# Seven block products per two batches in an attention and mixer kernel, with the last weights rounded a pair earlier

## The chip, the cores and the metric

The kernel runs on one core of a Trainium2 chip. The time is device microseconds (us) of one execution. Engines are named as in the profile: PE (matmuls), PEld (PE's weight loads), DVE (VectorE), ACT (ScalarE), POOL (GpSimd) and SP, whose queue issues nearly all transfers. Each engine works through its own queue in order and waits on semaphores that other engines raise.

## The reference

```python
def _attn_ref(q, k, v, centroids):          # batch 4, 8 heads, 768 tokens, head size 64
    ...
    mask = q_assign[:, :, :, None] == k_assign[:, :, None, :]
    scores = scale * np.matmul(q, k.transpose(0, 1, 3, 2))
    scores = np.where(mask, scores, -1000000000.0)
    ...
    return np.matmul(attn, v).astype(np.float32)

def _moe_ref(x, w_tok1, w_tok2, w_ch1, w_ch2):   # 768x256, 256x768, 512x1536, 1536x512
    xt = x.transpose(0, 2, 1)
    h = np.maximum(xt @ w_tok1, 0.0) @ w_tok2
    u = x + h.transpose(0, 2, 1)
    h2 = np.maximum(u @ w_ch1, 0.0) @ w_ch2
    return (u + h2).astype(np.float32)
```

Everything is float32. The output of the attention, with the heads side by side, is the `x` (768 tokens by 512) of the mixer.

## The kernel before

The program has three stretches, all written out by hand in one order; nothing is reordered afterwards, so the text of the program is the order of each engine's queue.

**Attention** (up to about 318 us): 16 pairs of heads, `g` = 0 to 15, four pairs for each batch. Of a pair, PE makes scores (line 422), ACT the exponentials (429), DVE adds them up (437), PE multiplies with v (447), ACT copies the result out (454), a transposing transfer turns it (459), and in the next pair ACT puts it into `x` (`pair_put`, 472) and DVE divides (`pair_out`, 498). Beside this the mixer's weights are loaded and rounded (`weight_steps`), in pieces of 128 by 512 words of 8 bytes. One piece is: a load into `raw` on SP (197), two ACT operations (203: `wh`, 205: `wup`), three DVE operations (210, 215, 220, the last writing `wT`), and an integer add on POOL (227) that writes the weight. A step of the list takes the load of piece i, the ACT part of piece i-1 and the rest of piece i-2. The first three weights (19 pieces) are finished in pair 14; the 12 pieces of the last one, `ch2`, begin in pair 15.

**Tokens** (318 to 401 us). `tok1(b, t)`: six matmuls of 512 columns into one bank (527), then a ReLU into `h1s[b][:, t]`, in turn on DVE (512) and ACT (514). `tok2(b, j)`: two matmuls of 512 columns (536), and DVE adds the bank into `xs[b][:, j]` (539). There are 8 calls of the first and 24 of the second. They run in the order of the list `ends`: `tok1` of batches 0 and 1, `tok2` of batch 0, `tok1` of batch 2, `tok2` of batch 1, `tok1` of batch 3, `tok2` of batches 2 and 3. Between them stand the remaining steps of `ch2`'s rounding and the four sums of `left_weights` (550, 553; 1536 elements each), then the steps that transpose batch 0's `x` for the next stretch: `u_take` (ACT copy 597, transposing transfer 599) and `u_put` (ACT copy 610). `u_sums` (four DVE operations of 768 elements) stands at the end.

**Channels** (401 us to the end), batch by batch. Both products are made by `chunk`: a 2-by-2 block product from seven block products (Winograd's form) with the sums S1 to S4 of the left blocks and T1 to T4 of the right ones. Of one chunk the products into the three banks X, Z and Y stand in this order on PE, and an engine reads a bank out after every product:

```python
X: A11*B11 | X of the chunk before: A22*T4 (late) | Z: S1*T1 | Y: A12*B21
X += S2*T2 | Z += S4*B22 | X += S3*T3
```

With `last`, Y stands after `X += S2*T2`, and Z after `X += S3*T3`. A product that adds to X or Z may begin only when the read of the product before in that bank has ended. In `ch1_chunk` a product is two matmuls of 384 columns (689); ACT copies `p1`, `p5` and `u2` out (697), DVE adds the others and makes the next product's sums (553, 710, 714, 550). In `ch2_chunk` a product is three matmuls of 256 columns (740), and DVE makes all seven reads. `right_weights` (four DVE operations of 1536 elements) follows the first two chunks of the first batch.

Of the kernel before, what the change touches and what calls it, by code (L numbers as in the profile page):

```python
# [19 lines left out]
P = 128  # L20
NJ = S // P
DM = H * D
# [26 lines left out]
def kernel(  # L49
# [131 lines left out]
    def weight_steps(pool, W, names):  # L181

        def tmp(name, dt, n):  # L190
            bufs = 1 if name == "wT" else 2
            return pool.tile([P, WMAX], dt, tag=name, name=name, bufs=bufs)[:, 0:n]

        def load_bits(src, p):
            n = p["n"] = src.shape[1]
            raw = pool.tile([P, WMAX, 2], U32, tag="raw", name="raw", bufs=3)[:, 0:n]
            nc.sync.dma_start(raw.rearrange("p n two -> p (n two)"), src.bitcast(U32))
            p["lo"], p["hi"] = raw[:, :, 0], raw[:, :, 1]

        def scalar_part(p):  # L200

            p["h"] = tmp("wh", U32, p["n"])
            nc.scalar.activation(out=p["h"].bitcast(F32), in_=p["hi"].bitcast(F32), func=ACT.Abs)
            p["up"] = tmp("wup", I32, p["n"])
            nc.scalar.activation(out=p["up"], in_=p["lo"], func=ACT.Copy, scale=float(2.0**-29))

        def rest(dst, p):

            h = p["h"]
            nc.vector.tensor_scalar(  # L210
                out=h.bitcast(F32), in0=h.bitcast(F32), scalar1=TINY, scalar2=HUGE,
                op0=ALU.max, op1=ALU.min,
            )

            nc.vector.tensor_scalar(  # L215
                out=h, in0=h, scalar1=0x07FFFFFF, scalar2=3,
                op0=ALU.bitwise_and, op1=ALU.logical_shift_left,
            )
            T = tmp("wT", U32, p["n"])
            nc.vector.scalar_tensor_tensor(  # L220
                out=T, in0=p["hi"], scalar=0xC0000000, in1=h,
                op0=ALU.bitwise_and, op1=ALU.bitwise_or,
            )
            T, up = T.bitcast(I32), p["up"]
            if len(dst.shape) == 3:
                T, up = (y.rearrange("t (p j) -> t p j", j=NJ) for y in (T, up))
            nc.gpsimd.tensor_tensor(out=dst.bitcast(I32), in0=T, in1=up, op=ALU.add)  # L227

        pieces = list(weight_pieces(W, names))
        parts = [{} for _ in pieces]  # L230
        for i in range(len(pieces) + 2):

            def step(i=i):
                if 2 <= i:
                    rest(pieces[i - 2][0], parts[i - 2])
                if 1 <= i <= len(pieces):
                    scalar_part(parts[i - 1])
                if i < len(pieces):
                    load_bits(pieces[i][1], parts[i])

            yield step
# [265 lines left out]
    turns = [0, 0]  # L507

    def relu(dst, src):
        turns[0] += 1  # L510
        if turns[0] % 2:
            nc.vector.tensor_scalar_max(out=dst, in0=src, scalar1=0.0)
        else:
            nc.scalar.activation(out=dst, in_=src, func=ACT.Relu)

    def mtile(shape, name):
        turns[1] += 1
        return pools["ps_m"].tile(shape, F32, tag="XZ"[turns[1] % 2], name=name)
# [3 lines left out]
    def tok1(b, t):  # L522
        if t == 0:
            h1s[b] = tokpool.tile([P, NT, DM], F32, name="h1", bufs=2)
        pf = mtile([P, DM], "ph1")
        for j in range(NJ):
            nc.tensor.matmul(  # L527
                pf, lhsT=W["tok1"][:, j, t * P : (t + 1) * P], rhs=xs[b][:, j],
                start=(j == 0), stop=(j == NJ - 1),
            )  # L530
        relu(h1s[b][:, t], pf)

    def tok2(b, j):
        pu = mtile([P, DM], "pu")
        for t in range(NT):
            nc.tensor.matmul(  # L536
                pu, lhsT=W["tok2"][:, t, j], rhs=h1s[b][:, t], start=(t == 0), stop=(t == NT - 1)
            )
        nc.vector.tensor_tensor(out=xs[b][:, j], in0=pu, in1=xs[b][:, j], op=ALU.add)  # L539
# [15 lines left out]
    def left_weights():  # L555
# [3 lines left out]
        A = {  # L559
# [6 lines left out]
        yield lambda: add(A["S1"], A["A21"], A["A22"])  # L566
        yield lambda: sub(A["S2"], A["S1"], A["A11"])
        yield lambda: sub(A["A21"], A["A11"], A["A21"])
        yield lambda: sub(A["S4"], A["A12"], A["S2"])
        A["S3"] = A["A21"]  # L570
        pools["A"] = A

    def right_weights():
# [7 lines left out]
        extra = pools["wsums"].tile([P, 3, NCT // 2, DM // 2], F32, name="w2s")  # L581
# [38 lines left out]
    def u_sums():  # L620
        uT = pools["uT"]
        uTs = pools["uTs"] = pools["u"].tile([P, 3, NF // 2, HS], F32, name="uTs")
        R = {"B11": uT[:, 0, 0:2], "B21": uT[:, 0, 2:4], "B22": uT[:, 1, 2:4]}
        R["T1"], R["T2"], R["T4"] = (uTs[:, i] for i in range(3))
        R["T3"] = b12 = uT[:, 1, 0:2]
        sub(R["T1"], b12, R["B11"])
        sub(R["T2"], R["B22"], R["T1"])
        sub(R["T3"], R["B22"], b12)
        sub(R["T4"], R["B21"], R["T2"])
        pools["R"] = R  # L630
# [3 lines left out]
    def chunk(n, product, done, last=False):  # L634
# [39 lines left out]
        late.append(end)  # L674

# [165 lines left out]
    ends = [lambda t=t: tok1(0, t) for t in range(NT)]  # L841
    for b in range(B):
        if b + 1 < B:
            ends += [lambda b=b, t=t: tok1(b + 1, t) for t in range(NT)]
        ends += [lambda b=b, j=j: tok2(b, j) for j in range(NJ)]

# [10 lines left out]
    for g in range(NPAIR):  # L857
        final = g == NPAIR - 1
        if final:
            assert not weights  # L860
            routing.close()
            W["ch2"] = pool("wc2pool", 1, side="right").tile([P, NCT, DM], F32, name="wc2")
            weights = list(weight_steps(stage, W, ("ch2",)))
# [17 lines left out]
        rounding(1)  # L881
        for qh in range(2):
            values(g, qh)
# [11 lines left out]
        rounding(final or g % 2 == 0 and 0 < g < EARLY)  # L895
# [3 lines left out]
    for m in range(9):  # L899
        ends.pop(0)()  # L900
        if m == 1:
            pair_put(NPAIR - 1)
            pair_out(NPAIR - 1)
        if m % 3 == 2:
            rounding(2)
    assert not state
    attention.close()
    pools["wsums"] = pool("wsums", 1, side="right")
    pools["u"] = pool("upool", 1, side="right")
    beside = weights + list(left_weights())  # L910
    turning = list(u_steps(0))
    while ends:
        for _ in range(-(-len(beside) // len(ends))):
            beside.pop(0)()
        ends.pop(0)()
        if len(ends) < 18 and turning:
            turning.pop(0)()
    u_sums()
    staging.close()
    tokens.close()  # L920
    pools["mlp"] = pool("mlp", 1)
    beside = list(right_weights())
    for b in range(B):
        for part in range(2):
            for i in range(3):
# [6 lines left out]
                for _ in range(2):  # L932
                    if beside:
                        beside.pop(0)()
# [10 lines left out]
            if part == 1 and b + 1 < B:  # L945
                u_sums()
# [217 lines left out]
```

## Time and profile before

| what | us |
|---|---|
| median of 3 runs (lowest, highest) | 845.09 (844.76, 845.1) |
| profiled execution | 844.87 |
| its span | 843.0 |
| PE matmul busy | 833.0 |
| DVE busy | 501.5 |
| ACT busy | 375.0 |
| POOL busy | 45.7 |
| scores from `qkT`, line 422, 768 records | 155.1 |
| exponentials on ACT, line 429, 192 | 149.2 |
| sums on DVE, line 437, 128 | 127.7 |
| POOL's integer adds into `wc`, 128 by 512, line 227, 24 | 33.0 (mean 1.376) |

How to read it: a float32 matmul leaves two records in the profile, so 96 records are 48 matmuls; matmuls are pipelined, so a record is longer than the distance to the next one. In the lines below, a time in square brackets is how long the engine sat idle before, and behind the arrow stands what ended it. `128x512 f32` is partitions by elements. Times in a timeline are counted from the start of the span.

### The profile page before, as it was taken

Reading aid. Unit: us, or ns where it says so; the run is one execution under the profiler, and the core shown is the slowest. Engines: PE = TensorE matmul, PEld = TensorE weight load, DVE = VectorE, ACT = ScalarE, POOL = GpSimd, SP = SyncE. Lnnn points to the kernel's source line nnn. Section 1 sums busy time; section 2 is a strip of 40 time slices with the busy share of each in tenths; the row PEclk is TensorE's granted clock in tenths of the full one; section 3 lists DMA queues with packets and bytes.
Section 4 is the critical chain, followed back from the end, with each engine's and each line's share of the span. In section 5 each row is a group of like instructions: output and inputs, shape, how many; then the busy total and the mean of one; then the engine's idle time right before and its main releaser. Section 6 shows DMA issues by size and latency. Waiting matters only on the chain.

```text
span 843.0 us, 10784 instructions
## 1 busy us (share of the span) xinstructions
PE 833.0 (99%) x4102; PEld 506.3 (60%) x4102; DVE 501.5 (59%) x848; ACT 375.0 (44%) x570; POOL 45.7 (5%) x40
## 2 busy tenths in 40 slices
PE   8999999999999999999999999999999999999997
PEld 4444444444444444444577686785876867768676
DVE  6879898989898862893653434423454333443342
ACT  5678677777777762453210352103612035220210
POOL 1001010101101000330000000000000000000000
PEclk9999999999999999999999999999999999999999
DMA  9887566867775312541000050000310012200001
GB/s 152 152 149 150 114 138 136 164 129 156 149 134 122 57 44 71 170 101 28 0 1 1 19 107 26 0 1 19 87 46 0 1 19 47 85 1 0 1 17 63
DMA packets 183963, 60.19 MB, mean 71 GB/s; under 512 B 172768, under 2 KB 176864, under 8 KB 183904
## 3 DMA queue, kind: packets, MB, share of 16 engines
q1 hardware_dynamic: 182304, 59.04, 33.2%
q8 instruction: 34, 0.56, 0.3%
q10 hardware_dynamic: 1600, 0.39, 0.2%
q14 instruction: 25, 0.20, 0.1%
HBM read 34.64 MB, written 6.29 MB: 49 GB/s over the span
## 4 chain that ended last, share of the span: by engine, by line
PE 92%; DVE 6%; issue 0%; ACT 0%; DMA 0%; DVEq 0%
PE sc L422 18%; PE pX L740 15%; PE pX L689 15%; PE av L447 13%; PE pZ L689 7%; PE pZ L740 7%; PE ph L527 4%; PE pY L740 4%; PE pY L689 4%; PE pu L536 3%; PE small L483 1%; DVE wh L215 1%; PE small L302 1%; DVE wT L220 1%; DVE wh L210 1%; DVE sum L437 1%
## 5 line engine op out<-in xcount | busy, mean ns | idle before, releaser
L429 ACT ACTIVATE ex<-sc 128x768 f32<-128x768 f32 x192 | 149.2, 812 | 27.6 <-PE sc L422 16.1
L422 PE MATMUL sc<-qkT 64*128 64x384 f32 x768 | 155.1, 482 | 0.0
L437 DVE TENSOR_TENSOR sum<-sum,ex 128x768 f32<-128x768 f32 x128 | 127.7, 997 | 27.4 <-ACT ex L429 15.2
L447 PE MATMUL av<-ex,va 128*64 128x384 f32 x768 | 127.4, 488 | 0.0
L447 PEld LDWEIGHTS av<-ex,va 128*64 128x64 f32 x768 | 53.7, 137 | 71.7 <-issue 67.9
L422 PEld LDWEIGHTS sc<-qkT 64*128 64x128 f32 x768 | 68.4, 187 | 36.3 <-issue 35.5
L697 ACT COPY p<-pX 128x384 f32<-128x384 f32 x24 | 11.4, 475 | 139.5 <-PE pX L689 121.2
L689 PE MATMUL pX<-uT,wc 128*128 128x384 f32 x192 | 67.4, 487 | 0.0
L422 PE MATMUL sc<-ohT 64*128 64x384 bf16 x384 | 63.3, 324 | 0.5 <-DVE ohT L394 0.2
L689 PEld LDWEIGHTS pX<-uT,wc 128*128 128x128 f32 x192 | 36.2, 190 | 24.7 <-issue 1.0
L454 ACT COPY avrows<-av 128x768 uint16<-128x768 uint16 x32 | 25.5, 798 | 47.1 <-PE av L447 47.1
L227 POOL TENSOR_TENSOR wc<-wT,wup 128x512 int32<-128x512 int32 x24 | 33.0, 1376 | 191.3 <-DVE wT L220 191.3
L527 PE MATMUL ph<-x,wt 128*128 128x512 f32 x96 | 41.9, 594 | 0.8 <-DVE x L539 0.8
L610 ACT COPY uT<-ucols 128x768 uint16<-128x768 uint16 x32 | 33.7, 1052 | 19.7 <-DMA ucols<-urows 19.7
L536 PE MATMUL pu<-h,wt 128*128 128x512 f32 x96 | 41.7, 592 | 0.0
L422 PEld LDWEIGHTS <-ohT 64*128 64x128 bf16 x384 | 20.1, 94 | 35.9 <-issue 11.1
L553 DVE TENSOR_TENSOR c<-pZ,u 128x384 f32<-128x384 f32 x24 | 13.4, 557 | 46.9 <-PE pZ L689 46.9
L708 ACT ACTIVATE hA<-hA 128x384 f32<-128x384 f32 x24 | 12.6, 523 | 63.4 <-DVE hA L553 63.4
L553 DVE TENSOR_TENSOR x<-pX,x 128x256 f32<-128x256 f32 x24 | 10.2, 423 | 42.8 <-PE pX L740 42.8
L689 PE MATMUL pZ<-uTs,w1s 128*128 128x384 f32 x96 | 35.0, 487 | 0.4 <-DVE uTs L550 0.4
L740 PE MATMUL pX<-wc,hA 128*128 128x256 f32 x144 | 35.0, 379 | 0.0
L740 PE MATMUL pZ<-w2s,hS 128*128 128x256 f32 x144 | 35.0, 379 | 0.0
(121 smaller groups left out, 1222.3 us busy)
## 6 DMA issues: line engine op xcount, KB each, us to landing
raw<-in_moe_w_ch_dram SPq DMA_DIRECT2D x24, 512.0 KB, 4.2
va<-in_v_dram SPq DMA_DIRECT2D x16, 384.0 KB, 3.6
out_dram<-x SPq DMA_DIRECT2D x24, 256.0 KB, 2.2
qk<-in_k_dram SPq DMA_DIRECT2D x60, 96.0 KB, 3.9
qk<-in_q_dram SPq DMA_DIRECT2D x60, 96.0 KB, 3.5
raw<-in_moe_w_tok_dram SPq DMA_DIRECT2D x3, 512.0 KB, 4.3
raw<-in_moe_w_tok_dram SPq DMA_DIRECT2D x4, 384.0 KB, 3.8
ucols<-urows SPq DMA_TRANSPOSE x32, 2.8
```

Of the source, the lines that this page charges most:

```text
L227: nc.gpsimd.tensor_tensor(out=dst.bitcast(I32), in0=T, in1=up, op=ALU.add)
L422: nc.tensor.matmul(sc[:, h, 0:HS], lhsT=src[rows, 1, j], rhs=src[rows, 0, js], start=start, stop=not start,)
L429: nc.scalar.activation(out=ex, in_=sc[:, :, 0:HS], func=ACT.Exp, scale=SM_SCALE)
L437: nc.vector.tensor_tensor(out=acc, in0=acc if j > 1 else st["ex", qh, 0], in1=st["ex", qh, j], op=ALU.add)
L447: nc.tensor.matmul(av[h * D : (h + 1) * D], lhsT=st["va"][:, h, j], rhs=ex[:, h], start=(j == 0), stop=(j == NJ - 1),)
L454: nc.scalar.copy(out=st["rows"][:, qh], in_=av.bitcast(U16).rearrange("p (t w) -> p w t", w=2))
L527: nc.tensor.matmul(pf, lhsT=W["tok1"][:, j, t * P : (t + 1) * P], rhs=xs[b][:, j], start=(j == 0), stop=(j == NJ - 1),)
L536: nc.tensor.matmul(pu, lhsT=W["tok2"][:, t, j], rhs=h1s[b][:, t], start=(t == 0), stop=(t == NT - 1))
L553: nc.vector.tensor_tensor(out=dst, in0=a, in1=b, op=ALU.add)
L610: nc.scalar.copy(out=out, in_=pools.pop(("ucols", i)).rearrange("p w j t -> p w (j t)"))
L689: nc.tensor.matmul(psum, lhsT=A[a][:, k, c * P : (c + 1) * P], rhs=R[r][:, k], start=start and k == 0, stop=k == 1, skip_group_check=not s ...
L740: nc.tensor.matmul(psum, lhsT=h2[a][:, k, i * P : (i + 1) * P], rhs=Bw[w][:, 3 * part + k], start=start and k == 0, stop=k == 2, skip_grou ...
```

## The change

**The second token product** is made with `chunk` too. Two batches b and b+1 are the two columns of the right matrix: the blocks B are `h1s[b][:, 0]`, `h1s[b+1][:, 0]`, `h1s[b][:, 1]`, `h1s[b+1][:, 1]`; the blocks A are the quarters of `tok2`'s weight (token half by row, `t` by column). A product is one matmul of 512 columns, a chunk has 7, and there are 3 chunks for each two batches. DVE adds every one of the seven reads into `xs` directly. `token_weights` makes S1 to S4 of the weight (4 operations of 384 elements), `token_sums` T1 (after the ReLU of `tok1(b+1, 0)`) and T2, T3, T4 (after that of `tok1(b+1, 1)`), 512 elements each. All ReLUs are on ACT.

**The rounding**: ACT's `up` is written over `raw`'s low words, DVE's line 220 over `wh`; `wT` and `wup` are gone, `raw` has 4 buffers in place of 3, `wh` 2. For `ch2` the loads run two steps ahead of ACT's part (`ahead=2`), and the integer add is on DVE (as an instruction on halves of words, 128 by 1024) in place of POOL. Its first step is in the middle of pair 14, two at its end, two in the middle of pair 15 and one at its end; 9 remain for the tokens.

**The order of the tokens.** First batches 0 and 1: `tok1(0,0)`, a rounding step, `pair_put` and `pair_out` of pair 15, `token_weights`; `tok1(0,1)`, two steps; `tok1(1,0)`, T1, one step; `tok1(1,1)`, T2, T3, T4; three chunks. Then batches 2 and 3: `tok1(2,0)`, two `u_take`, two rounding steps; `tok1(2,1)`, two steps, two pairs of `u_put` and `u_take`; `tok1(3,0)`, T1, the last step, the first sixth of `left_weights`; `tok1(3,1)`, T2, T3, T4, two pairs of `u_put` and `u_take`; three chunks, with the other `u_put`s between them and the first two of `u_sums` between the second and the third chunk. The other two of `u_sums` follow.

**The sums of the channel weights**: `left_weights` is made in six parts of 256 elements by four operations. The first is made with the tokens, part c+1 after `ch1` chunk c of the first batch, ahead of the operations of `right_weights`, of which two follow chunk 0 and two chunk 1.

```diff
-    def weight_steps(pool, W, names):
+    def weight_steps(pool, W, names, ahead=1, adder=nc.gpsimd):
...
-            raw = pool.tile([P, WMAX, 2], U32, tag="raw", name="raw", bufs=3)[:, 0:n]
+            raw = pool.tile([P, WMAX, 2], U32, tag="raw", name="raw", bufs=4)[:, 0:n]
...
-            p["up"] = tmp("wup", I32, p["n"])
+            p["up"] = p["lo"].bitcast(I32)
...
-            T = tmp("wT", U32, p["n"])
             nc.vector.scalar_tensor_tensor(
-                out=T, in0=p["hi"], scalar=0xC0000000, in1=h,
+                out=h, in0=p["hi"], scalar=0xC0000000, in1=h,
...
-            nc.gpsimd.tensor_tensor(out=dst.bitcast(I32), in0=T, in1=up, op=ALU.add)
+            adder.tensor_tensor(out=dst.bitcast(I32), in0=T, in1=up, op=ALU.add)
...
-                if 2 <= i:
-                    rest(pieces[i - 2][0], parts[i - 2])
-                if 1 <= i <= len(pieces):
-                    scalar_part(parts[i - 1])
+                if ahead < i:
+                    rest(pieces[i - ahead - 1][0], parts[i - ahead - 1])
+                if ahead <= i < len(pieces) + ahead:
+                    scalar_part(parts[i - ahead])
...
-        relu(h1s[b][:, t], pf)
-
-    def tok2(b, j):
-        pu = mtile([P, DM], "pu")
-        for t in range(NT):
-            nc.tensor.matmul(
-                pu, lhsT=W["tok2"][:, t, j], rhs=h1s[b][:, t], start=(t == 0), stop=(t == NT - 1)
-            )
-        nc.vector.tensor_tensor(out=xs[b][:, j], in0=pu, in1=xs[b][:, j], op=ALU.add)
+        nc.scalar.activation(out=h1s[b][:, t], in_=pf, func=ACT.Relu)
...
+    def left_sums(A, part):
+        a = {name: part(x) for name, x in A.items()}
+        yield lambda: add(a["S1"], a["A21"], a["A22"])
+        yield lambda: sub(a["S2"], a["S1"], a["A11"])
+        yield lambda: sub(a["S3"], a["A11"], a["A21"])
+        yield lambda: sub(a["S4"], a["A12"], a["S2"])
...
+    def token_sums(b, t):
...
+        if t == 0:
+            sub(R["T1"], R["B12"], R["B11"])
+        else:
+            sub(R["T2"], R["B22"], R["T1"])
+            sub(R["T3"], R["B22"], R["B12"])
+            sub(R["T4"], R["B21"], R["T2"])
...
+    def tok2_chunk(b, i):
...
+        def product(psum, a, r, start):
+            nc.tensor.matmul(
+                psum, lhsT=A[a][:, i], rhs=R[r], start=start, stop=True,
+                skip_group_check=not start,
+            )
+
+        def done(name, psum):
+            x = u[to.get(name, name)]
+            add(x, psum, x)
+
+        chunk(DM, product, done, i == HJ - 1)
+        if i == HJ - 1:
+            late.pop()()
...
+        if g == NPAIR - 2:
+            assert not weights
+            routing.close()
+            W["ch2"] = pool("wc2pool", 1, side="right").tile([P, NCT, DM], F32, name="wc2")
+            weights = list(weight_steps(stage, W, ("ch2",), 2, nc.vector))
+            rounding(1)
+        rounding(g == NPAIR - 1)
...
+        for i in range(HJ):
+            tok2_chunk(b, i)
+            if b == 2 and i < 2:
+                take(turning, 2)
+            if b == 2 and i == 1:
+                u_sums(0)
...
+                if b == 0:
+                    c = 3 * part + i + 1
+                    for sums_of in left_chunk(c) if c < NCT // 2 else ():
+                        sums_of()
+                    take(others, min(len(others), 2))
```

## The prediction

> **What bounds the kernel now.** I read the page's busy times first, then the groups of the token stretch, the timeline of PE there, and what DVE did where PE stood.
>
> ```profile
> PE 833.0 (99%) x4102; PEld 506.3 (60%) x4102; DVE 501.5 (59%) x848; ACT 375.0 (44%) x570; POOL 45.7 (5%) x40
> L527 PE MATMUL ph<-x,wt 128*128 128x512 f32 x96 | 41.9, 594 | 0.8 <-DVE x L539 0.8
> L536 PE MATMUL pu<-h,wt 128*128 128x512 f32 x96 | 41.7, 592 | 0.0
> L539 DVE TENSOR_TENSOR x<-pu,x 128x512 f32<-128x512 f32 x24 | 16.3, 687 | 16.9 <-PE pu L536 16.9
> ```
>
> PE is the bound all through, so a removed matmul is worth its full length and every new wait of PE costs its full length.
>
> ```profile
> 348.94 10.46 PE L527 MATMUL ph<-x,wt 128*128 128x512 f32 x24
> 359.24 10.46 PE L536 MATMUL pu<-h,wt 128*128 128x512 f32 x24
> 370.45 10.57 PE L527 MATMUL ph<-x,wt 128*128 128x512 f32 x24 [0.75 <-DVE x L539]
> 380.86 20.76 PE L536 MATMUL pu<-h,wt 128*128 128x512 f32 x48
> 401.46 1.45 PE L689 MATMUL pX<-uT,wc 128*128 128x384 f32 x4
> 403.27 1.56 PE L689 MATMUL pZ<-uTs,w1s 128*128 128x384 f32 x4 [0.36 <-DVE uTs L550]
> 404.66 1.45 PE L689 MATMUL pY<-uT,wc 128*128 128x384 f32 x4
> ```
>
> Start to start, 12 matmuls of 512 columns take 359.24 - 348.94 = 10.30, so 0.858 each; a pair of 384 columns takes 1.29 (404.66 to the next start, 405.95). The two waits cost more than their brackets. From 359.24 the next group was due at 369.54 and came at 370.45 (0.91), and then took 10.41 to the next start in place of 10.30: 1.02 lost. At 403.27, due at 402.75, 0.52 and 0.10: 0.62 lost. So a wait of PE costs its length past the due time and about 0.11 more.
>
> ```profile
> 369.71 0.68 DVE L539 TENSOR_TENSOR x<-pu,x 128x512 f32<-128x512 f32 x1
> 382.77 0.69 DVE L539 TENSOR_TENSOR x<-pu,x 128x512 f32<-128x512 f32 x1 [2.55 <-PE pu L536]
> 402.26 0.95 DVE L550 TENSOR_TENSOR uTs<-uT 128x768 f32<-128x768 f32 x1
> ```
>
> An add starts 0.19 after its matmuls' due end (380.86 + 2 x 0.858 = 382.58, start 382.77), takes 0.69, and PE starts 0.06 after it (370.39 to 370.45). Adds in a row follow at 0.61.
>
> **Removed.** Of 48 matmuls of the second product 42 stay: -6 x 0.858 = -5.15. The wait at 370.45 goes: the add it waited for was late behind rounding and 1.7 to 2.5 us long sums, which no longer stand there: -1.02. The one at 403.27 goes, because T1 is made before the last chunk: -0.62. Together -6.79.
>
> **Added inside the chunks.** Twice in a chunk (`X += S3*T3` after `X += S2*T2`, and the late product after that) only one matmul, 0.858, lies between a product and the next one in the same bank, which must wait for the read: 0.19 + 0.69 + 0.06 = 0.94. That is 0.08 late, with the 0.11 it is 0.19; 12 times: +2.28. No row shows PE waiting so briefly: without the 0.11 it is 0.08 each (1.0), with a restart twice as dear 0.30 (3.6). I take the middle, which both rows have.
>
> **At the first chunk of each two batches** `X += S2*T2` needs the read of `p1`, which DVE takes after T2, T3 and T4. For batches 0 and 1: PE ends `tok1(1,1)` at 317.93 + 24 x 0.858 = 338.5; the ReLU (0.59) ends at 339.3; T2 to T4 at 0.61 each, then the read, end at 341.9; PE was due three products later, at 341.1: +0.94 with signal and restart.
>
> **At the last chunk** `X += S2*T2` comes one product earlier, and DVE reads the late product of the chunk before first. After the late product's end 0.19, 0.61, 0.69, 0.06 make 1.55 against 0.858, with restart +0.80. For batches 2 and 3 the two operations of `u_sums` (0.95 each) stand ahead of both reads: counted from the former chunk's end the read ends at 3.97, with signal and restart 4.14, and PE was due at 2.76: +1.38 in place of 0.80.
>
> **Batches 2 and 3, first chunk.** Here queues are late one behind the other. PE (with the stalls so far) ends `tok1(2,0)` at 364.6, `(3,0)` at 374.9, `(3,1)` at 380.0. The two `u_take` follow the ReLU on ACT (0.75 each). SP has their two transposing transfers ahead of the loads of pieces 10 and 11; these took 1.25 each at 367.19, so the loads leave at 368.6 and land 3.7 later (the median of the loads in this stretch), 372.3. ACT's part of the two pieces (1.2 each) ends at 374.7, two `u_put` with `u_take` (1.7 each) at 378.1, and only then comes the ReLU of `tok1(3,0)`, to 378.7. DVE waits for it with T1 (379.3) and has behind it the last piece (2.4, to 381.7), the sixth of `left_weights` (4 operations of 256, 0.42 each, to 383.2), T2 to T4 and the read: 385.7, with signal and restart 385.9. Due was 382.6: +3.3. Ends: 0.94, if nothing is late, and 4.4.
>
> A piece on DVE is taken from these rows:
>
> ```profile
> 334.30 0.42 DVE L210 TENSOR_SCALAR wh<-wh 128x512 f32<-128x512 f32 x1
> 334.75 0.43 DVE L215 TENSOR_SCALAR wh<-wh 128x512 uint32<-128x512 uint32 x1
> 335.26 0.69 DVE L220 SCALAR_TENSOR_TENSOR wT<-raw,wh 128x512 uint32<-128x512 uint32 x1
> 336.33 1.41 DVE L215 TENSOR_SCALAR wh<-wh 128x512 uint32<-128x512 uint32 x1
> ```
>
> The last one shares its time with a POOL add (336.18 to 337.45), which the change takes out of this stretch. The integer add on DVE is in no row. From below: 0.69, line 220 on 512 words with the same strided operand. From above: POOL's 1.38 for the same add. I take 0.8, near the row of the same engine and words: 0.45 + 0.51 + 0.69 + 0.75 start to start, 2.4 for a piece. With 1.38 the same walk through the queues gives 1.73 and 4.4 for the two first chunks in place of 0.94 and 3.3, +1.9.
>
> **The channel weights in sixths.** Part c+1 stands behind the chunk's last operations, and the next chunk's `S1*T1` needs it.
>
> ```profile
> 411.11 1.45 PE L689 MATMUL pX<-uTs,wc 128*128 128x384 f32 x4
> 412.40 0.81 PE L689 MATMUL pZ<-uTs,w1s 128*128 128x384 f32 x2
> ```
> ```profile
> 410.02 0.56 DVE L553 TENSOR_TENSOR hA<-pX,p 128x384 f32<-128x384 f32 x1 [0.66 <-PE pX L689]
> 411.17 0.56 DVE L714 SCALAR_TENSOR_TENSOR hS<-c,hA 128x384 f32<-128x384 f32 x1
> 411.76 0.56 DVE L550 TENSOR_TENSOR hS<-hS,hA 128x384 f32<-128x384 f32 x1
> 412.24 1.75 DVE L550 TENSOR_TENSOR w2s<-wc 128x1536 f32<-128x1536 f32 x1
> ```
>
> The new S1 takes the place of the operation at 412.24; with 0.42 (the mean for 256 elements) it is done at 412.66, and PE wanted it at 412.40: 0.32 late with the signal, 0.43 with the restart. After chunks 2 and 5 `ch2` chunks come between, so four times: +1.72 (ends 1.3 and 2.2).
>
> **Costed at nothing.** In pairs 14 and 15 ACT gets three pieces of 1.3 and DVE two of 2.4 ahead of pair 15's denominators (318.07 becomes 319.8), and the copies and the transposing transfer of pair 15, on SP behind two more loads, move some 2 us, `pair_put` to about 326. They feed `tok1(3,0)` at 369.9, over 40 us of cover; the first `tok1` began at 317.93, before the denominators were read, so it needs nothing of them. A piece of ACT work ahead of the exponentials stood at the end of pairs 2 to 12 too, and line 422's 768 records waited 0.0. `token_weights` (4 x 0.56) and, in the first two batches, four pieces end on DVE before 338, T1 before 336; PE asks for T1 at 339.4. Four more ReLUs (0.59) on ACT fall where it waits for PE anyway. POOL's adds of the first 19 pieces now read `raw` with a stride and hold `raw` and `wh` longer; even at twice 1.38 the next add starts 4.56 later at the closest (261.57 and 266.13) and a `wh` comes up two adds later, so no queue sees it. The two operations of `right_weights` (1.75 each) end 7.4 after a chunk's end, before the next `c12` is read (8.4). If that cover were gone, a read would be late by the overlap, under 1 us twice.
>
> The granted clock was 1.00 in each stretch here, with no wait over 1.2. [...]
>
> **Sum.** -6.79 + 2.28 + 0.94 + 0.80 + 3.3 + 1.38 + 1.72 = +3.6. The profiled execution, 844.87, becomes 848.5; the median of the runs is 0.2 above it: 848.7.
>
> **Rivals.** *Short waits cost nothing*: if PE holds its next matmul ready and a read frees the bank within 0.86, the 2.28 and the 1.72 fall away: 844.7, not slower. For it: weight loads run ahead of the matmuls; against it: both waits shown paid 0.11 more, and 0.94 is over 0.86. *No backlog*: if the second two batches stall like the first (0.94), as when pieces 10 and 11 land by 369, 846.3; against it is SP's order. *Both*: 842.4, the only way to be clearly faster. *A slow integer add*, 1.38: 850.6; for it is that POOL needs that long, against it DVE's rate on 512 words.
>
> **How the numbers follow.** Forecast 0.47, short waits 0.19, no backlog 0.14, both 0.08, slow add 0.12. The likeliest has its own range from 847.0 to 850.5. The low ends of all terms give 844.7, the high ends 852.4; from 844.5 to 851.0 leaves out the faster case and the top. A measurement here can tell about 0.2%, 1.7 us, from no change: faster 0.08 + 0.01 = 0.09; within it 0.19 and half of 0.14, 0.26; slower the rest, 0.65.
>
> **What would show it.** In the profile after: 84 records of the second product; PE waits on DVE's add into `x` of some 3.3, 1.4, 0.9 and 0.8 just ahead of `X += S2*T2`; four waits of 0.3 for `w1s`; no wait at the first `tok1` of batch 3. A DVE queue empty at the second two batches' first chunk, or matmuls 0.858 apart throughout a chunk, would make the forecast wrong.

## The result, and the profile after

| | before | after |
|---|---|---|
| median of 6 runs each (lowest, highest) | 845.1 (844.76, 845.74) | 854.4 (852.84, 855.55) |
| profiled execution, its span | 844.87, 843.0 | 854.64, 852.9 |
| first `tok1` product starts | 317.93 | 320.29 |
| first channel product starts | 401.46 | 408.03 |
| first product of `ch2_chunk` starts | 428.29 | 437.18 |

The changed kernel is slower by 1.06%: the ratio is 1.0106, interval 1.0093 to 1.0119. The direction was forecast, the size was not: +9.3 us where the sum had +3.6, and 854.4 where the range ended at 851.0.

The last three rows of the table say where the 9.9 us of the two spans arose: 2.36 in the attention, where the forecast had nothing; 4.21 in the tokens (87.74 in place of 83.53), where it had 2.5; 2.32 in the first channel part and 1.01 behind it, where it had 1.1 for both.

From the page of after, the busy times; then the list of PE's waits (total, how often, the longest).

```profile
PE 834.5 (98%) x4090; PEld 504.2 (59%) x4090; DVE 520.0 (61%) x906; ACT 374.3 (44%) x574; POOL 30.6 (4%) x28
```
```profile
PE pX L702 <- DVE x L536: 5.5, 4, 3.2
PE sc L420 <- ACT ex L427: 2.2, 4, 0.6
PE pX L728 <- ACT u L736: 2.0, 2, 1.0
PE pZ L728 <- DVE w1s L536: 0.2, 1, 0.2
```

PE has 12 records, six matmuls, fewer and yet is busy longer: in place of 1.02, single products below took 1.94 and 1.91 where the granted clock had fallen, and 1.12 to 1.13 behind waits. Of the list, the first line is what the prediction was about. The second and the third it had costed at nothing.

PE in the tokens, line 702 being a token block product (one matmul, two records), at the first and last chunks:

```profile
342.71 1.02 PE L702 MATMUL pY<-h,wt 128*128 128x512 f32 x2
344.37 1.13 PE L702 MATMUL pX<-h1s,wt2s 128*128 128x512 f32 x2 [0.64 <-DVE x L536]
345.33 1.02 PE L702 MATMUL pZ<-h,wt2s 128*128 128x512 f32 x2
346.28 1.98 PE L702 MATMUL pX<-h,wt 128*128 128x512 f32 x4
348.19 1.12 PE L702 MATMUL pX<-h1s,wt 128*128 128x512 f32 x2
...
355.54 1.02 PE L702 MATMUL pZ<-h1s,wt2s 128*128 128x512 f32 x2
357.09 1.12 PE L702 MATMUL pX<-h1s,wt2s 128*128 128x512 f32 x2 [0.52 <-DVE x L536]
...
384.19 1.02 PE L702 MATMUL pY<-h,wt 128*128 128x512 f32 x2
388.41 1.94 PE L702 MATMUL pX<-h1s,wt2s 128*128 128x512 f32 x2 [3.20 <-DVE x L536]
390.14 1.91 PE L702 MATMUL pZ<-h,wt2s 128*128 128x512 f32 x2
391.85 1.96 PE L702 MATMUL pX<-h,wt 128*128 128x512 f32 x4
...
401.08 1.02 PE L702 MATMUL pZ<-h1s,wt2s 128*128 128x512 f32 x2
403.25 1.13 PE L702 MATMUL pX<-h1s,wt2s 128*128 128x512 f32 x2 [1.14 <-DVE x L536]
```

Read starts, not lengths. After 342.71 the next start was due 0.858 later, at 343.57; it came at 344.37, 0.80 late, and the one after it took 0.96 in place of 0.86: 0.90. In the same way the others give 0.79, 3.36 and 1.41. And after the longest wait the next two starts are 1.73 and 1.71 apart, twice the 0.86, and TensorE's granted clock was 0.50 from 389 to 392. The windows of four us (busy time of PE, PEld, DVE, ACT and POOL with the number of records, granted clock, DMA share, GB/s) show it:

```profile
382.00:386.00 4.00, 3.21 (x8) 1.14 (x6) 3.86 (x10) 3.33 (x5) 0.00 (x0) 1.00 0.26 49
386.00:390.00 4.00, 1.59 (x2) 0.71 (x3) 3.54 (x6) 2.77 (x4) 0.00 (x0) 0.82 0.52 98
390.00:394.00 4.00, 4.00 (x8) 1.55 (x7) 2.08 (x3) 2.19 (x3) 0.00 (x0) 0.75 0.92 86
```

An account of the stretch: 48 products of `tok1` and 42 token block products at 0.858 are 77.2, and the stretch is 87.74, so 10.5 are lost. The four waits are 6.46 of it, the two slow products 1.72 and the rest, 2.3, is the short waits inside the chunks: in the rows above, 345.33 to 346.28 is 0.09 too long, the two products from 346.28 to 348.19 are 0.19 too long and the start of the next product (349.15) comes 0.10 late, 0.38 a chunk. Before, 96 products made 82.4 and 1.2 were lost.

The wait of 3.20 has the chain of queues behind it that the prediction walked through. ACT, then DVE:

```profile
375.23 0.68 ACT L202 ACTIVATE wh<-raw 128x512 f32<-128x512 f32 x1 [2.26 <-DMA raw<-in_moe_w_ch_dram]
380.88 0.62 ACT L522 ACTIVATE h<-ph 128x512 f32<-128x512 f32 x1
```
```profile
381.53 0.69 DVE L533 TENSOR_TENSOR h1s<-h,h 128x512 f32<-128x512 f32 x1 [3.16 <-ACT h L522]
```

ACT waits for the late load, the ReLU of `tok1(3,0)` stands behind two pieces and two pairs of copies, T1 waits for the ReLU, and behind T1 stand the last piece, the sixth, T2 to T4 and at last the read.

### The profile page after: what moved, and what is told of

Its sections match the earlier page's. It is cut to its first block, busy times and chain, and to the rows that moved or that the text cites. A ratio compares the mean times of both kernels' runs of the same rounds, so it can differ in the third digit from the quotient of the medians.

```text
span 852.9 us, 10831 instructions
## 1 busy us (share of the span) xinstructions
PE 834.5 (98%) x4090; PEld 504.2 (59%) x4090; DVE 520.0 (61%) x906; ACT 374.3 (44%) x574; POOL 30.6 (4%) x28
## 4 chain that ended last, share of the span: by engine, by line
PE 90%; DVE 5%; ACT 2%; issue 1%; DMA 0%; DVEq 0%; ACTq 0%
PE sc L420 17%; PE pX L779 15%; PE av L445 14%; PE pX L728 13%; PE pZ L779 7%; PE pZ L728 7%; PE pY L779 4%; PE pY L728 3%; PE ph L518 3%; PE pX L702 2%; PE small L481 1%; PE small L300 1%; PE pZ L702 1%; PE av L852 1%; DVE x L536 1%
## 5 line engine op out<-in xcount | busy, mean ns | idle before, releaser
L536 DVE TENSOR_TENSOR x<-pX,x 128x512 f32<-128x512 f32 (+1 forms) x48 | 26.4, 556 | 51.4 <-PE pX L779 42.8
L779 PE MATMUL pX<-w2s,hA 128*128 128x256 f32 x144 | 35.0, 379 | 0.0
L779 PE MATMUL pY<-wc,hA 128*128 128x256 f32 x144 | 35.0, 379 | 0.0
```

What stands on the lines that cost most here:

```text
L536: nc.vector.tensor_tensor(out=dst, in0=a, in1=b, op=ALU.add)
L779: nc.tensor.matmul(psum, lhsT=h2[a][:, k, i * P : (i + 1) * P], rhs=Bw[w][:, 3 * part + k], start=start and k == 0, stop=k == 2, skip_grou ...
```

## The experiments

Each kernel was measured against the kernel before on the same chip. Edits are to the changed kernel unless said otherwise. The cause of each of the three stretches was tested by itself, then all fixes together, then the price of a wait.

### Attention: a third buffer for `wh`

ACT at the end of pair 2, in after:

```profile
71.15 0.68 ACT L202 ACTIVATE wh<-raw 128x512 f32<-128x512 f32 x1 [1.68 <-POOL wt L225]
71.72 0.67 ACT L204 ACTIVATE raw<-raw 128x512 int32<-128x512 uint32 x1
72.28 6.78 ACT L427 ACTIVATE ex<-sc 128x768 f32<-128x768 f32 x9
```

The same place in the kernel before, where `wT` was a tile of its own:

```profile
69.31 0.68 ACT L203 ACTIVATE wh<-raw 128x512 f32<-128x512 f32 x1 [0.25 <-DVE wT L220]
70.74 0.68 ACT L205 ACTIVATE wup<-raw 128x512 int32<-128x512 uint32 x1 [0.74 <-POOL wt L227]
71.31 2.90 ACT L429 ACTIVATE ex<-sc 128x768 f32<-128x768 f32 x4
```

`wh` now holds the result that POOL adds, so ACT may write it only when POOL is done. ACT waited for POOL before the change too, but at its second operation (0.74, for `wup`); now it waits ahead of the first, so that one operation more, 0.57 from start to start, comes after the wait. The exponentials behind it start 1 us later (0.4 of it because this whole execution runs 0.4 later, from ahead of the first score product on), and PE, which needs them, waits:

```profile
73.13 0.34 PE L420 MATMUL sc<-ohT 64*128 64x384 bf16 x2 [0.56 <-ACT ex L427]
```

```diff
-            return pool.tile([P, WMAX], dt, tag=name, name=name, bufs=2)[:, 0:n]
+            return pool.tile([P, WMAX], dt, tag=name, name=name, bufs=3)[:, 0:n]
```

> The changed kernel with a third buffer for wh; all else the same. Theory: in the changed kernel POOL's add still reads wh when ACT wants the buffer two pieces later (ACT waits of 1.7 for POOL in the even pairs, and four waits of PE of 0.54 for an exponential after them); with a third buffer these go, and the first token product starts some 2.0 us sooner (320.3 becomes 318.0 to 318.4): time 852 to 852.7 in place of 854.4. Rival: the attention starts later by chance of the first transfers, and the buffer does not matter: no change beyond 0.5 us, and the four waits of 0.54 stay.

Measured: 851.49 (849.86 to 852.01), ratio to before 1.0069 (1.0053 to 1.0086). PE's four waits on `ex` are gone, the first `tok1` starts at 317.14, and the waits on reads in the tokens stay what they were (5.5 in all). So this one buffer is worth 2.9 of the 9.3. The timelines agree, and they divide it: from the first score product of one pair to that of the next, the four pairs take 19.83 to 19.85 in after, 19.28 to 19.35 before and 19.12 with the third buffer. The kernel before thus lost some 0.2 in each of them already; the change added 0.5 to 0.6 in each, 2.0 in all. The other 0.39 of the 2.36 stands ahead of the first score product (10.24 before, 10.63 after), where the profiled executions of kernels with the same opening lie between 10.15 and 11.12.

### Channels: four trials at one wait

In after, DVE, ACT and PE around the first wait on `u` (line 736 is ACT's copy, 740 its ReLU on the first block, 728 the product):

```profile
419.65 1.75 DVE L533 TENSOR_TENSOR w2s<-wc 128x1536 f32<-128x1536 f32 x1
421.44 1.76 DVE L533 TENSOR_TENSOR w2s<-wc,w2s 128x1536 f32<-128x1536 f32 x1
...
423.58 0.55 DVE L536 TENSOR_TENSOR hA<-pY,p 128x384 f32<-128x384 f32 x1
```
```profile
424.17 0.52 ACT L740 ACTIVATE hA<-hA 128x384 f32<-128x384 f32 x1 [3.44 <-DVE hA L536]
424.59 0.46 ACT L736 COPY u<-pX 128x384 f32<-128x384 f32 x1
```
```profile
422.63 1.45 PE L728 MATMUL pZ<-uT,w1s 128*128 128x384 f32 x4
425.11 2.85 PE L728 MATMUL pX<-uT,wc 128*128 128x384 f32 x8 [1.02 <-ACT u L736]
```

Follow it backwards: PE's `X += S3*T3` was due at 423.92 and waits for the copy of `u2`. That copy needed only a product that had begun at 421.34, but in ACT's queue it stands behind a ReLU, which waits for DVE's add of `c11`, which stands behind a sixth of the left sums and two right sums. It happens twice (1.19 and 1.15 late, each with some 0.1 behind it): 2.5. The sixths themselves made PE wait four times, 0.31 and 0.10 each, as at 418.66 (due at 417.06 + 1.29 = 418.35):

```profile
418.66 1.56 PE L728 MATMUL pZ<-uTs,w1s 128*128 128x384 f32 x4
```

**The right sums one at a time**

```diff
     others = list(right_weights())
+    take(others, 1)
...
-                    take(others, min(len(others), 2))
+                    take(others, min(len(others), 1))
```

> The changed kernel with the four sums of the last weight taken one before the first channel chunk and one after each of its first three, in place of two and two. Theory: PE's two waits for ACT's copy of u2 (due 423.9, came 425.1; due 434.7, came 435.8) come from DVE being full: two sums of 1.75 and a sixth of 1.5 push the add c11, ACT's ReLU waits for it, and the copy of u2 stands behind the ReLU. Both go, 2.3 to 2.5 us less: about 852.0. The waits of 0.4 for w1s stay (4 times). Rival: the copies are late from ACT's own load; the waits stay, time within 0.5 of 854.4.

Measured: 853.84 (853.74 to 854.25), ratio 1.0102 (1.0086 to 1.0119). The two waits are gone and the part takes 26.64 in place of 29.15, but a wait of 1.2 on DVE's read `p` stands at the first `ch2` chunk instead. That is neither the 852.0 of the theory nor the rival, in which the two waits stay: the loss has moved.

**Each sixth a chunk earlier**

```diff
+                if b == 0:
+                    c = 3 * part + i + 1
+                    for sums_of in left_chunk(c) if c < NCT // 2 else ():
+                        sums_of()
                 ch1_chunk(part, i)
...
-                    c = 3 * part + i + 1
-                    for sums_of in left_chunk(c) if c < NCT // 2 else ():
-                        sums_of()
```

> The changed kernel with the sixth of the channel weights' sums for chunk c+1 taken before chunk c in place of after it; the same operations, one chunk sooner. Theory: the four waits for w1s (0.31 and 0.10 restart each) go, 1.6 us less, about 852.8, and the two waits for u2 stay, since DVE has as much between two chunks as before. Rival: it is the sixths that make DVE late for u2 as well, by where they stand; then those 2.5 go too, about 850.3.

Measured: 853.8 (851.84 to 854.45), ratio 1.0094 (1.0077 to 1.0111). The waits on `w1s` are gone, those on `u` stayed, as expected, but grew from 2.0 to 2.8 in all, and this part takes 29.15 as before; the expected 852.8 did not come.

**The right sums on GpSimd**, with the early sixths:

```diff
-        yield lambda: sub(B_["T1"], B_["B12"], B_["B11"])
+        yield lambda: sub(B_["T1"], B_["B12"], B_["B11"], nc.gpsimd)
...
-    others = list(right_weights())
+    take(list(right_weights()), 4)
```

> The four right sums of the channel weights go from VectorE to GpSimd, all issued ahead of the first channel chunk, and each sixth of the left sums is issued ahead of the chunk before its own. Theory (VectorE is full in the first channel part: the right sums make the ReLU chain late, the sixths make the products late): both waits on ScalarE's u, 2.5 together, and the four waits on w1s, 1.7, go: 854.4 - 4.2 = 850.2 (849.5 to 851). Rival 1 (GpSimd takes over 8 us for one, 32 us for the four): T1 and T2 come late and the first channel-two chunk waits, 852 or more. Rival 2 (the two earlier trials gave little because the waits in this part only move): 853.5 or more.

Measured: 863.99 (862.03 to 864.97), ratio 1.0225 (1.0208 to 1.0242), slower than after by 9.6 us. Both rivals allowed such a time, neither for this cause: GpSimd was done at 422.0, 23 us before the first `ch2_chunk` (445.44), and DVE was late. POOL, then DVE, in this kernel:

```profile
406.63 3.54 POOL L533 TENSOR_TENSOR w2s<-wc 128x1536 f32<-128x1536 f32 x1 [104.88 <-PE pX L702]
...
414.28 4.17 POOL L533 TENSOR_TENSOR wc<-wc 128x1536 f32<-128x1536 f32 x1
418.41 3.59 POOL L533 TENSOR_TENSOR w2s<-wc,w2s 128x1536 f32<-128x1536 f32 x1
```
```profile
407.10 3.88 DVE L533 TENSOR_TENSOR uT<-uT 128x768 f32<-128x768 f32 x1
...
415.09 3.63 DVE L536 TENSOR_TENSOR w1s<-wc 128x256 f32<-128x256 f32 x1
418.76 3.52 DVE L533 TENSOR_TENSOR w1s<-w1s,wc 128x256 f32<-128x256 f32 x1
422.20 0.41 DVE L533 TENSOR_TENSOR wc<-wc 128x256 f32<-128x256 f32 x1
```

The DVE sums run one beside each POOL sum and end 0.3 to 0.8 after it: a sum of 256 elements takes 3.5 to 3.6 while POOL works and 0.41 as soon as it has stopped, at 422.00. PE stood 11.5 us, by the chain above: the add of `c11` stands behind these sums (422.87), ACT's ReLU and its copy of `u2` behind the add.

**ACT's ReLU behind its copy**, with the early sixths; all sums on DVE:

```diff
             if name in ("p1", "p5", "u2"):
...
                 nc.scalar.copy(out=kept[name], in_=psum)
+                if name == "u2":
+                    a = h2["A11"][:, i]
+                    nc.scalar.activation(out=a, in_=a, func=ACT.Relu)
             elif name == "c11":
                 a = h2["A11"][:, i]
                 add(a, psum, kept["p1"])
-                nc.scalar.activation(out=a, in_=a, func=ACT.Relu)
```

> In a channel chunk ScalarE's ReLU on the first block is issued behind its copy of u2 instead of ahead of it, and the sixths of the left sums are issued a chunk early; VectorE keeps all its sums. Theory (TensorE waits for a copy of u2 which is itself ready, but stands in ScalarE's queue behind a ReLU that waits for VectorE): both waits on ScalarE's u (2.0, 2.5 with their restarts) and the four on w1s (1.7) go: 854.4 - 4.2 = 850.2 (849.7 to 851.2). Rival (VectorE itself is full, so what is late only shows at the next place): 853 or more, with a wait of about 1 us in the first channel-two chunk, as with the spread right sums.

Measured: 849.51 (848.44 to 850.78), ratio 1.0048 (1.0031 to 1.0065): 4.9 less than after, where 4.2 was expected, and 4.3 less than with the early sixths alone. All waits of this part are gone, and from the first channel product to the first of `ch2_chunk` it takes 25.80 in place of 29.15 (26.83 before the change). So DVE was not full; the order of one engine's queue made it look so, and both the sixths and the right sums are free once ACT's copy does not stand behind them.

### Tokens: the first sixth behind the first reads

```diff
-            take(list(left_chunk(0)), 4)
...
             tok2_chunk(b, i)
+            if b == 2 and i == 0:
+                take(list(left_chunk(0)), 4)
```

> The changed kernel with the first sixth (four operations of DVE, 1.46 us) taken after the first token chunk of batches 2 and 3 in place of ahead of T2. Theory with the clock: the wait of PE before its first S2*T2 there falls from 3.2 to about 1.7, and the two matmuls after it, which took 1.73 and 1.71 from start to start in place of 0.86, run at the full rate again: 1.46 + 1.72 = 3.2 us less, about 851.2. Rival: the two slow matmuls have another cause (they wait for DVE, or the clock falls anyway after a wait of 1.7): 1.5 less, about 852.9. If the reads of the second chunk now come late, up to 0.3 is given back.

Measured: 852.29 (851.33 to 853.08), ratio 1.0085 (1.0068 to 1.0101). The wait fell from 3.20 to 1.86, nearly by the 1.46 of the four operations that no longer stand ahead of the read, and in the profiled execution the products after it kept their full rate (0.96 and 0.95 to the next starts, a granted clock of 1.00 from 386 to 394): the stretch took 84.98 in place of 87.74. Two of the four executions were some 1.5 slower than the other two (with a granted clock of 0.997 and below against 0.998 and above); this comes back below.

### Tokens: eight products

```diff
+    def tok2(b, j):
+        pu = mtile([P, DM], "pu")
+        for t in range(NT):
+            nc.tensor.matmul(
+                pu, lhsT=W["tok2"][:, t, j], rhs=h1s[b][:, t], start=(t == 0), stop=(t == NT - 1)
+            )
+        add(xs[b][:, j], pu, xs[b][:, j])
...
-            take(list(token_weights()), 4)
...
-            tok2_chunk(b, i)
+            for j in range(4 * i, 4 * i + 4):
+                tok2(b + j // NJ, j % NJ)
```

(T1 to T4 of the tokens are left out with it.)

> This kernel undoes the product alone: eight block products per chunk as before, two matmuls an output and one read, no token weight sums and no T1 to T4; the rounding in place, the order of the queues, the sixths and the right sums stay as in the changed kernel (854.4). Theory (the seven-product form costs more in waits on its reads than its six matmuls save): the stretch of the token products is 87.74 us in the changed kernel; without any wait it would be 76.7 with seven products and 81.9 with eight, so the stretch falls by some 5.8 although the kernel has 5.15 more of matmuls, and the time is 848.6 (848 to 850). Rival (the loss in this stretch comes from the rounding and the queues, not from sums and reads): the waits of 3.2 and 1.9 and the slow clock behind them stay, and the time is 853.5 or more.

Measured: 849.5 (849.14 to 849.86), ratio 1.0051 (1.0035 to 1.0068). There is no wait of PE left in the tokens, and the stretch takes 82.50, against 82.4 for its 96 products without any wait. So the seven products, in the order in which they were put, cost 4.9 us net by the medians and 5.2 by the stretch: they save 5.15 and lose 10.4. The rounding, the queues of SP and ACT and the sixth ahead of the reads all stayed, and cost PE nothing here. Two things differ: an output takes its bank again only after three others (four banks in turn, 1.72 an output), so a read may be some 5 us late; and DVE has 24 reads in place of 42 and none of the sums. This run does not part the two; the next one keeps every read and sum.

### Tokens: three chunks woven

```diff
+    ORDER = (
+        "X0 X1 Y0 Y1 Z0 X2 Z1 X0 X1 Z0 X2 Z1 X0 X1 Z2 X2 X0 X1 Y2 Z2 X2"
+    ).split()
...
-        token_sums(b, 1)
...
+        beside = {1: [lambda: token_sums(b, 1)], 5: [lambda: token_sums(b, 2)], 8: [lambda: token_sums(b, 3)]}
+        if b == 2:
+            beside[6] = beside[13] = [lambda: take(turning, 2)]
+            beside[18] = [lambda: u_sums(0)]
+        tok2_woven(b, beside)
```

Letter and number are a bank and its chunk, each bank's products in their old order, a read behind every product; `beside` names the work issued behind the read of that number. T2, T3 and T4 stand there one by one.

> The three chunks of a token pair are woven into one order of 21 products, in which a bank that is read is used again only after two other products at least, and T2, T3, T4 and the first two of u's sums stand behind reads in VectorE's queue instead of ahead of them. The first product that needs a read comes seven products (6 us) after the first. Same matmuls, same reads, same sums. Theory (all of the loss in this stretch is waits on reads that are late): the tight waits of 2.3, the 0.9, 0.8, 1.4 and 3.2 and the slow clock of 1.7 behind it go, the stretch falls from 87.74 towards 76.7, the time to 843.5 (843 to 846). Rival (VectorE becomes the bound: 21 reads of 0.69 and three sums of 0.68 are 16.5 us of the 18.0 that 21 products take, with sixths and u's sums 20 in the second pair): some 4 us stay, 847.5 or more.

Measured: 846.14 (845.65 to 846.61), ratio 1.0009 (0.9999 to 1.0019). PE's list of waits has one line left for the tokens, and the stretch takes 79.25. PE in this kernel (line 738 is the product), at the first chunk of batches 2 and 3:

```profile
383.75 1.02 PE L738 MATMUL pZ<-h1s,wt2s 128*128 128x512 f32 x2
386.21 1.13 PE L738 MATMUL pX<-h,wt 128*128 128x512 f32 x2 [1.44 <-DVE x L536]
387.17 1.02 PE L738 MATMUL pZ<-h1s,wt2s 128*128 128x512 f32 x2
```

The late queues of batches 2 and 3 are still late, but five products stand between them and PE. The sixth, X2, takes the bank of Y0 and so waits for that read; the expectation had seven products ahead of the first that needs a read. Behind the wait the products are 0.86 apart, and so is all of batches 0 and 1: 18.1 us for 21 products, with DVE busy for 15.1 of them. DVE is no bound there. The expected 843.5 was too low by the 1.7 of this wait with its restart and by 0.5, because 76.7 for a stretch without waits was 77.2 when counted in products; 846.14 lies 0.14 above the expected range.

### All together, on GpSimd

The weave, the third buffer, all right sums and all six sixths on GpSimd, the sixths issued in the second token pair.

> The weave, the third buffer of wh, and on GpSimd all 24 left sums of the channel weights (issued in the second token pair) and the four right sums. If the three causes add: 854.4 - 10.9 (weave) - 2.9 (wh) - 4.2 (channels) = 836.4 (836 to 839), faster than the kernel before by 0.7 to 1.1%. If GpSimd's 24 sums of about 0.75 are not done before the first chunk needs its sixth, or VectorE is the bound in the tokens: 840 to 843.

Measured: 857.03 (849.9 to 857.98), ratio 1.0117 (1.0069 to 1.0166). The expected 836.4 did not come, and neither did its rival. Of DVE's sums of 768 elements, 0.95 to 0.96 alone, one took 3.10 beside the first of GpSimd's right sums (four, 3.40 to 4.19 each, from 401.33 on), and the next began beside the second and ended only after the fourth (416.46):

```profile
406.26 11.02 DVE L533 TENSOR_TENSOR uTs<-uT,uTs 128x768 f32<-128x768 f32 x1
```

PE stood 11.1 at the first channel chunk. The sixths had nothing to wait for in GpSimd's queue and ran at 326 to 349, in the first token pair; DVE's rounding came late there, the reads behind it too, and PE waited 4.0 for one. So this kernel says nothing on the weave; it shows the long sums beside GpSimd's again.

### All together, on VectorE

The weave, the third buffer, the late ReLU, the early sixths, and the first sixth and u's sums behind later reads:

```diff
+            beside[11] = [lambda: take(left0, 2)]
+            beside[16] = [lambda: u_sums(0)]
...
+    take(left0, 2)
     u_sums(1)
```

> The weave, the third buffer of wh, the late ReLU, the early sixths, and the first sixth issued behind twelve of the 21 reads in place of ahead of them; all sums on VectorE. If the causes add: 846.1 (weave) - 2.9 (wh) - 2.5 to 4.2 (channels) - 1.5 (the weave's last wait) = 837.5 to 839.2, faster than the kernel before by 0.7 to 0.9%. If VectorE is full in the second token pair (21 reads, three T sums, a sixth and u's sums are 20.1 us of 18.0): 840 to 842, with waits of 2 us on reads there or on w1s and uTs at the first channel chunk.

Measured: 837.05 (836.95 to 837.52), ratio to before 0.9907 (0.989 to 0.9923). This is the version that beats both kernels: 17.3 us under the change and 8.0 under the kernel before. PE's whole list of waits:

```profile
PE av L887 <- DVE warm L874: 1.2, 1, 1.2
PE small L300 <- DVE qkT L290: 0.5, 1, 0.5
PE pr L300 <- ACT qkT L897: 0.2, 1, 0.2
PE sc L420 <- DVE ohT L392: 0.2, 1, 0.2
```

All four stand in the attention, and the changed kernel has them too. The tokens take 77.72, of which 77.2 are products; against the kernel before, 5.8 of the 7.9 us of the spans are won there, 1.0 in the first channel part and 1.0 ahead of the tokens (0.9 of it what the third buffer gives in pairs where the kernel before lost time too).

### The price of one wait

To the last kernel, one wait of PE is added in batches 0 and 1: T2 is computed five or eight times in place of once.

```diff
+        if b == 0:
+            beside[1] = 5 * beside[1]
```

> The kernel of the sum (837.05) with T2 of the first token pair written five times in place of once, so that VectorE's reads come 4 x 0.6 = 2.4 us later and TensorE, which has some 0.4 in hand there, waits once for about 2.0. Theory A (a wait costs its length, and about 0.1 to start again; the clock falls only for a wait of some 3 us or more): 839.1 (838.9 to 839.5), the executions close together. Theory B (the clock falls after shorter waits too, in some executions): some executions at 840.5 to 841, the others at 839.1.

> The same with T2 written eight times: reads 7 x 0.6 = 4.2 us later, one wait of about 3.8. Theory A: its length, a restart, and a stretch of half clock after it that costs 1.7, in every execution: 837.05 + 3.9 + 1.7 = 842.7 (842.3 to 843.2). If a wait costs its length alone: 840.9. If the slow stretch falls by chance: executions in two groups, 840.9 and 842.6.

Measured with five: 840.57 (839.73 to 841.62), ratio 0.9944 (0.9927 to 0.996), the four executions in two groups, 839.73 and 839.78, 841.36 and 841.62. With eight: 844.27 (843.39 to 844.8, ten executions), ratio 0.9988 (0.9978 to 0.9998). PE with five, in an execution of the slower group, then with eight:

```profile
344.89 1.67 PE L738 MATMUL pX<-h,wt 128*128 128x512 f32 x2 [2.31 <-DVE x L536]
...
348.06 2.23 PE L738 MATMUL pX<-h1s,wt2s 128*128 128x512 f32 x4
350.13 1.02 PE L738 MATMUL pZ<-h,wt2s 128*128 128x512 f32 x2
```
```profile
346.67 2.08 PE L738 MATMUL pX<-h,wt 128*128 128x512 f32 x2 [4.49 <-DVE x L536]
...
350.24 3.11 PE L738 MATMUL pX<-h1s,wt2s 128*128 128x512 f32 x4
353.19 1.02 PE L738 MATMUL pZ<-h,wt2s 128*128 128x512 f32 x2
```

With 2.31 of waiting, four products take 350.13 - 344.89 = 5.24 in place of 3.43: 1.8 more. With 4.49 they take 6.52: 3.1 more. So 837.05 + 2.31 + 1.8 = 841.2 and 837.05 + 4.49 + 3.1 = 844.6, which are the times of these executions (841.62 and 844.71) to 0.4 and 0.1; with five, the first score product of this execution came 0.4 later (10.55 against 10.15). Theory A fell for the shorter wait (half of the executions paid the clock too, by their times and, in the profiled one, by its trace), and its 1.7 was too little for some of the longer one's.

## Why the prediction was right, and where it failed

**Right, term by term.** *Removed*: six matmuls at 0.858 were worth 5.15: the kernel with eight products takes 82.50 in the tokens and the one with seven and hardly a wait 77.72, 4.8 apart, with 0.4 more lost in the second. *At the first chunk*: 0.94 for batches 0 and 1, measured 0.90; 3.3 for batches 2 and 3, measured 3.36. *At the last chunk*: 0.80 and 1.38, measured 0.79 and 1.41. *Inside the chunks*: 2.28, measured 2.3, so the rival in which short waits cost nothing is out. *The sixths*: 1.72, measured 4 x 0.41 = 1.64. *The integer add on DVE*: 0.8 taken, 0.69 measured, the lower bound; the slow add is out. Their sum was +3.6. What the three errors below cost, and 0.4 at the start of the span, is the rest.

**Failed: "a `wh` comes up two adds later, so no queue sees it"** (under "Costed at nothing"). The sentence checked POOL's own queue and `raw`, but not who writes that buffer next: ACT does, a step ahead of that add, and in pairs with two rounding steps within the same pair, with the exponentials behind it. PE waited four times, 0.56 at most, and the attention became 2.0 longer by it; the third buffer gives back 2.9. The row that the prediction read for such work ahead of the exponentials, line 422's 768 records with no wait, could not show it: the same row has 0.0 in after too (line 420), since the wait falls on the product of `ohT` that stands ahead of them.

**Failed: the cover of the right sums, "before the next `c12` is read (8.4)"; "If that cover were gone, a read would be late by the overlap, under 1 us twice".** The 7.4 was right: the right sums ended at 423.20, 7.4 after the chunk's last product (414.48 + 1.29). But the first thing to be late was not `c12`; it was the add of `c11`, read earlier in the chunk, and its lateness passed through ACT's queue to a copy that had nothing to do with it. Measured 2.5; and the sequence of trials shows where the cause lay, since to move the sums of DVE gave 0.6 and to move the ReLU on ACT, with the sixths, 4.9.

**Failed: the price of the long wait, "a wait of PE costs its length past the due time and about 0.11 more".** Its rows could not show it: no wait before was over 1.2. Behind the wait of 3.20 another 1.72 was lost in the profiled execution, at a granted clock of 0.50. Not every execution seems to pay it: two of the six took 852.84 and 852.87 (granted clock 1.0 and 0.998), the other four 854.26 to 855.55 (0.995 to 0.998).

The three together are 2.0 + 2.2 + 1.7 (the second is the channels' 3.3 against the 1.1 forecast) = 5.9; with the 0.4 at the start of the span, 3.6 + 6.3 = 9.9, the difference of the spans. The likeliest case had the waits of the tokens right to 0.1 each; the range failed because none of its ends held a wait in the attention, a wait on ACT's copy or the price of the clock. For the right sums the text had named a price, and left it out of the sum.

## What to carry to other kernels

When an engine's result is written in place, ask which engine writes that buffer next and what stands behind that write in its queue; a tile freed later is a wait in another engine's queue (2.0 us here). A block product with fewer matmuls makes chains of product and read in one bank: with one other product between a product and the next in its bank, each such step lost 0.19 here; woven from three chunks, with two others or more between, the same products and reads lost next to nothing where DVE was not late already. And where an engine looks full, first see whether what is late is its own work or only something that stands behind a wait in a queue: reordering two instructions on ACT gave 4.3 us, moving sums between places on DVE 0.6, and moving four of them to GpSimd cost 10.

## What was not expected of the hardware

**The granted clock fell after a wait of 2.31 us, shorter than theory A's 3.** In the profiled execution with that wait it was 0.84, 0.50 and 0.81 in the windows of 2 us from 344 to 350, which makes, as an estimate, (0.16 + 0.50 + 0.19) x 2 / 0.50 = 3.4 us at 0.50; it fell about 0.5 after PE had begun again. Two of the four executions were about 1.7 us longer than the others. With a wait of 4.49 all ten executions had a granted clock of 0.994 to 0.996, against 0.998 to 1.0 without the added wait, and in the one profiled it was 0.97, three times 0.50, and 0.82 in the windows of 2 us from 344 on, by the same sum 6.8 us at 0.50, with 3.1 us lost. A wait of 1.44 was followed by full rate in its profile (products 0.86 apart), and its ten executions lie within 1.0 us. With 1.86 the four executions fell into two groups as well, but none of the slower ones was profiled. So by these runs a wait of some 2 us or more can cost some 1.7 us more. What settles it in one execution was not tried; waits of 3.2 in the changed kernel seem to have gone unpaid in two executions of six.

**Beside a sum on GpSimd, VectorE's sums took about as long as GpSimd's**: 3.5 to 3.6 us in place of 0.42 (GpSimd's own 4.17 and 3.59), and once 11.02 in place of 0.96. It was not confined to sums: in the kernel before, between 336 and 370, DVE's rounding operations with one input (lines 210 and 215) took 1.18 to 1.19 and 1.37 to 1.41 in place of 0.42 and 0.43 beside POOL's integer adds of 1.26 to 1.32. DVE's adds from a bank were not touched by it: there three in a row from 346.99 on took 1.88, 0.6 apart, beside POOL's add from 347.22 to 348.49; in the changed kernel, with POOL idle, two in a row took 1.29 (349.35). No run shows why.
